# An attention and bilinear feed-forward kernel: the last matrix product by Strassen's scheme, every engine's instructions in a written order

## The chip, the cores and the metric

The kernel runs on one core of one Trainium2 chip. The metric is the device time of one execution in microseconds, lower being better. Five engines run side by side from queues of their own: TensorE (PE; its weight loads are shown apart as PEld), VectorE (DVE), ScalarE (ACT), GpSimd (POOL) and SyncE (SP, which here only issues the transfers). They meet through semaphores.

## The reference

For 8 batches of 8 heads, 576 positions, head size 64, a softmax over 32 memory slots turns keys and values into 32 memory rows per head. The queries attend to these 32 rows. The result is read as a 4608 x 512 matrix `x` and goes through a feed-forward layer without a nonlinearity other than a product.

```python
a = phi - np.max(phi, axis=2, keepdims=True)
a = np.exp(a)
a = a / (np.sum(a, axis=2, keepdims=True) + 1e-09)
k_m = np.einsum('bhsm,bhsd->bhmd', a, k)
v_m = np.einsum('bhsm,bhsd->bhmd', a, v)
...
attn = attn / (np.sum(attn, axis=-1, keepdims=True) + 1e-09)
return np.matmul(attn, v_m).astype(np.float32)
...
a = x @ w1
b = x @ w2
h = a * b @ w3
return (h @ w_out).astype(np.float32)
```

`d_ff` is 1024 and the output has 512 columns. The weights come as float64.

## The kernel before

Three things are folded. `w3 @ w_out` is one 1024 x 512 matrix, formed once at the start (`product`, in START). The values' memory rows are multiplied with `w1` and `w2` per batch (`memory_weights`, four steps M), so that the probabilities multiply the outcome directly. And each large product is taken in three passes on float32r numbers that are split in a high and a low half: high x high, high x low, low x high. A split (`split`, L110) is a copy that rounds, on ACT (L111), and a subtraction on DVE (L112).

After START, which brings in and converts the weights and does the attention of batch 0, the program runs over 8 batches. A batch has two stages:

- **A, 16 units** (`ab_unit`, L428). A unit makes 128 of the 1024 columns of `a` and of `b` for one half of the positions (288): 6 matmuls into PSUM bank `a`, 6 into `b` (L440). ACT copies `a` out (L449), DVE multiplies it with `b` into `gr` (L451), and `gr` is split into `gh` and `gl` (L454).
- **O, 16 parts** (`out_part`, L457). For each half of the positions and each 128 of the 512 output columns, 24 matmuls (8 slices of the 1024, three passes, L465) add up in one PSUM bank `o`. ACT copies it to `osb` (L470) and SP sends it off.

The attention of the next batch is spread among the units. Its steps are named in the tables FIRST (batch 0) and STEADY (the others): `top` (maximum of phi, L158), `exp` (L164), `norm`, `turn0` and `turn4` (transposes on PE, L180 and L184, copied out by ACT), `mem` (L194), `blocks` (L219, then four small DVE instructions), `sc` (scores, L234), `se`, `sn`, `pr` (softmax and split), `M` (L293 and a split). `C` converts one piece of the weights from float64 with two ACT and three DVE instructions (L372 to L377), `N` is an M of batch 0, `K` splits a piece of `w3 @ w_out`.

PE and SP follow the order in which the program is written, that is, these tables. The order on ACT and DVE is set by the compiler's scheduler, which moves instructions by its own estimate of when they become ready. POOL does nothing after the first microsecond. PSUM has eight banks: `a` and `b` twice each, `o` twice, and a pair `x` for the small work.

## Time and profile before

| | |
|---|---|
| median of 3 runs | 556.19 us (554.48 to 556.4) |
| profiled execution, first to last instruction | 554.0 us |
| PE busy | 538.2 us (97%), 4696 matmuls |
| DVE busy | 311.4 us (56%), 599 instructions |
| ACT busy | 253.7 us (46%), 522 instructions |
| POOL busy | 0.7 us, 6 instructions |
| mean granted TensorE clock | 0.997 |

The profiled execution's own time is known as its span alone. What lies around it is taken as the difference to the median, 2.2 us. In the trace the first A unit starts at 75.1 us, batch 0 ends at 142.7 us, and the batches after it take 59.6 us each. Busy times add up durations that overlap: a 288-column matmul is shown with 295 ns, but the next one starts 133 ns after it.

### The profile page before, as it was taken

How to read it: one execution, taken by the hardware profiler on the slowest of the kernel's cores; microseconds unless marked ns; L12 is line 12 of the kernel's file. 1: busy time of each engine (PE TensorE's matmuls, PEld its weight loads, DVE VectorE, ACT ScalarE, POOL GpSimd, SP SyncE). 2: the span in 40 equal slices, each digit the busy share in tenths (PEclk: the TensorE clock that was granted, in tenths of full speed). 3: DMA queues.
4: the chain of work that ended last, by engine and by line, in shares of the span. 5: the costliest groups of instructions: out<-in, count | busy, mean ns of one | idle time of the engine just before them, and what ended most of it. 6: DMA issues, size and time to landing. Idle time of an engine off the chain costs nothing.

```text
span 554.0 us, 11182 instructions
## 1 busy us (share of the span) xinstructions
PE 538.2 (97%) x4696; PEld 470.1 (85%) x4696; DVE 311.4 (56%) x599; ACT 253.7 (46%) x522; POOL 0.7 (0%) x6
## 2 busy tenths in 40 slices
PE   3999989999999999999999999999999999999997
PEld 1453458988999899989998899989998999899997
DVE  5887997637457624681558335762478155824500
ACT  5877784624544434452543444333544354424411
POOL 0000000000000000000000000000000000000000
PEclk9999999999999999999999999999999999999999
DMA  8999628008140511333043304050123200110011
GB/s 316 407 372 391 254 76 297 4 24 300 64 158 27 168 37 38 136 118 95 4 172 99 96 22 164 22 170 33 70 104 128 87 2 2 34 44 11 1 44 44
DMA packets 28819, 64.17 MB, mean 116 GB/s; under 512 B 2144, under 2 KB 10336, under 8 KB 28768
## 3 DMA queue, kind: packets, MB, share of 16 engines
q1 hardware_dynamic: 28768, 63.45, 32.7%
q8 instruction: 37, 0.61, 0.5%
q14 instruction: 14, 0.11, 0.1%
HBM read 54.00 MB, written 9.44 MB: 115 GB/s over the span
## 4 chain that ended last, share of the span: by engine, by line
PE 91%; DVE 4%; DMA 2%; ACT 1%; issue 1%; DVEq 0%; ACTq 0%
PE o L465 37%; PE a L440 18%; PE b L440 18%; PE x L194 3%; PE a L387 2%; PE b L387 2%; PE a L293 2%; PE x L293 2%; DMA raw<-in_w_out 1%; PE x L180 1%; PE b L293 1%; PE x L234 1%; DVE w L377 1%; DMA raw<-in_w3T 1%; DVE w L376 1%; PE o L387 1%
## 5 line engine op out<-in xcount | busy, mean ns | idle before, releaser
L465 PE MATMUL o<-gh,Wh 128*128 128x288 f32 x512 | 152.9, 299 | 0.0
L465 PE MATMUL o<-gl,Wh 128*128 128x288 f32 x512 | 151.1, 295 | 0.0
L465 PE MATMUL o<-gh,Wl 128*128 128x288 f32 x512 | 151.1, 295 | 0.0
L465 PEld LDWEIGHTS o<-gh,Wh 128*128 128x128 f32 x512 | 96.8, 189 | 11.9 <-issue 11.9
L451 DVE TENSOR_TENSOR gr<-b,a_sb 128x288 f32<-128x288 f32 x128 | 58.5, 457 | 84.2 <-PE b L440 80.9
L111 ACT CAST gh<-gr 128x288 fp32r<-128x288 f32 x128 | 55.4, 433 | 99.4 <-DVE gr L451 99.4
L465 PEld LDWEIGHTS o<-gl,Wh 128*128 128x128 f32 x512 | 96.3, 188 | 0.0
L465 PEld LDWEIGHTS o<-gh,Wl 128*128 128x128 f32 x512 | 96.2, 188 | 0.0
L112 DVE TENSOR_TENSOR gl<-gr,gh 128x288 fp32r<-128x288 f32 x128 | 58.5, 457 | 56.7 <-ACT gh L111 56.4
L440 PE MATMUL b<-ah,mh 128*128 128x288 f32 x256 | 75.6, 295 | 2.7 <-DVE Wl L112 2.7
L440 PE MATMUL a<-ah,mh 128*128 128x288 f32 x256 | 78.0, 305 | 0.0
L440 PE MATMUL a<-al,mh 128*128 128x288 f32 x256 | 75.9, 296 | 0.0
L440 PE MATMUL b<-al,mh 128*128 128x288 f32 x256 | 75.9, 296 | 0.0
L440 PE MATMUL b<-ah,ml 128*128 128x288 f32 x256 | 75.9, 296 | 0.0
L440 PE MATMUL a<-ah,ml 128*128 128x288 f32 x256 | 75.8, 296 | 0.0
L470 ACT COPY osb<-o 128x288 f32<-128x288 f32 x64 | 25.3, 395 | 82.8 <-PE o L465 71.5
L449 ACT COPY a_sb<-a 128x288 f32<-128x288 f32 x128 | 50.5, 394 | 8.0 <-PE a L440 7.4
L440 PEld LDWEIGHTS a<-ah,mh 128*128 128x128 f32 x256 | 48.4, 189 | 4.2 <-issue 2.0
L440 PEld LDWEIGHTS b<-ah,mh 128*128 128x128 f32 x256 | 48.4, 189 | 3.0 <-DVE Wl L112 3.0
L440 PEld LDWEIGHTS b<-ah,ml 128*128 128x128 f32 x256 | 48.5, 189 | 0.0
L440 PEld LDWEIGHTS a<-ah,ml 128*128 128x128 f32 x256 | 48.5, 189 | 0.0
L440 PEld LDWEIGHTS b<-al,mh 128*128 128x128 f32 x256 | 48.4, 189 | 0.0
(89 smaller groups left out, 649.1 us busy)
## 6 DMA issues: line engine op xcount, KB each, us to landing
kv<-in_kv SPq DMA_DIRECT2D x16, 1024.0 KB, 7.8
q<-in_qT SPq DMA_DIRECT2D x8, 1152.0 KB, 6.0
outT<-osb SPq DMA_DIRECT2D x64, 144.0 KB, 1.8
raw<-in_w3T SPq DMA_DIRECT2D x7, 1024.0 KB, 11.9
ph<-in_phiT SPq DMA_DIRECT2D x8, 576.0 KB, 4.0
raw<-in_w SPq DMA_DIRECT2D x4, 1024.0 KB, 17.2
raw<-in_w_out SPq DMA_DIRECT2D x3, 1024.0 KB, 10.5
kv<-in_w SPq DMA_DIRECT2D x3, 1024.0 KB, 14.5
```

The source lines that it names most:

```text
L111: nc.scalar.copy(out=hi, in_=src)
L112: nc.vector.tensor_tensor(out=lo, in0=src, in1=hi.bitcast(F32), op=ALU.subtract)
L180: nc.tensor.transpose(ps[:, c, t], v["ph"][:, t, at : at + P], ident)
L194: nc.tensor.matmul(ps[h * M : (h + 1) * M, t, : 2 * D], lhsT=v["a"][:, i, t, h * M : (h + 1) * M], rhs=kvt[i][:, (4 * t + h) * 2 * D : (4 ...
L234: nc.tensor.matmul(ps[t][g * M : (g + 1) * M], lhsT=km[b % 2][t * D : (t + 1) * D, g], rhs=v["q"][t * D : (t + 1) * D, g, n * HALF : (n + ...
L293: nc.tensor.matmul(ps[t][g * M : (g + 1) * M], lhsT=vm[b % 2][d, g], rhs=w12_sb[q][d, :, g], start=True, stop=True,)
L387: nc.tensor.matmul(pw[r][i], lhsT=x[:, i * P : (i + 1) * P], rhs=wos[k // half][:, k % half], start=k == 0, stop=k == NF - 1,)
L440: nc.tensor.matmul(p, lhsT=x[:, t, w, fc : fc + P], rhs=y[:, n, t * HALF : (t + 1) * HALF], start=i == 0, stop=i == len(todo) - 1,)
L449: nc.scalar.copy(out=a_sb, in_=ps[0])
L451: nc.vector.tensor_tensor(out=gr, in0=ps[1], in1=a_sb, op=ALU.mult)
L465: nc.tensor.matmul(v["p"], lhsT=x[f // half][:, f % half, oc], rhs=y, start=f == 0 and i == 0, stop=f == NF - 1 and i == 2)
L470: nc.scalar.copy(out=osb, in_=v["p"])
```

## The change

**The O stage** is done by Strassen's scheme in Winograd's form. The 576 x 1024 matrix G of one batch (`a` times `b`) is cut in four quarters (two halves of the positions, two halves of the 1024), `w3 @ w_out` in four as well, and seven products of quarters take the place of eight. A product is two units of 12 matmuls (`out_unit`), so the stage has 14 units instead of 16 parts. The sums of quarters of G (16 subtractions or additions of 128 x 288 a batch) are done by POOL (`ab_unit`, `sums`), those of the weights, once, by POOL and DVE in batch 0 (`weights_of_out`: K, T, V, D, E, F, G). Sums of products are formed partly in PSUM, by further matmuls on the same bank, partly by four ACT copies (`keep`) and four DVE additions (`result`) of 128 x 576 a batch, which feed four transfers of 288 KB instead of eight of 144 KB.

**The splits** no longer follow each A unit: `gr` goes whole into G, and the operand of each O unit is split when it is near (`high_part` on ACT, h; `low_part` on DVE, l), 14 splits of 128 x 576 a batch in place of 16 of 128 x 288, through four buffers for each half.

**PSUM** is now four pairs of banks: `ab` twice, `o` and `x`. An A unit takes one pair, which comes free when its product with `b` is done.

**The order** of ACT, DVE and POOL is written out too, after START. Each unit has a group: what its batch needs, from the tables, and one group of STREAM, the next batch's attention, if a running estimate of DVE's backlog allows (`ahead_slot`). Two of the four M now stand in the O stage of the batch before, two in the A stage of their own.

**Conversions** C are cut in three, so that the last four lie between the first A units.

```diff
-STEADY = """
-A top A exp A norm A A turn0 A A turn4 A A mem A A kv2 blocks A A A A A
...
+BATCH_A = "A | A | A | A | A M | A h0 | A | A l0 | A M | A h1 | A l1 | A | A h2 | A | A l2 | A h3"
...
+BATCH_O = """
+O h4 l3 | O p1 h5 l4 | O h6 l5 | O p4 h7 l6 | O h8 l7 | O C11 h9 l8 | O h10 l9 | O u2 h11 l10 | O h12 l11 | O h13 p5 l12 |
...
+STREAM = """
+top | exp | norm turn0 | turn4 | mem | blocks kv | sc0 | mx0 | sb0 ex0 | sc1 q | sm0 | mu0 mx1 | tr0 sb1 ex1 | ah0 |
...
+LIMIT = 2100
...
+    def pair_ab():
+        return ps_ab.tile([P, 2, 512], F32, name="ab")
+
+    def pair_o():
+        return ps_ox.tile([P, 2, 512], F32, name="o")
+
+    def pair_x():
+        return ps_ox.tile([P, 2, 512], F32, name="x")
...
+            both = (pair_o(), pair_x()) if r else (pair_ab(), pair_ab())
+            pw[r] = [x[:, i] for x in both for i in range(2)]
...
-    def keep(r, i):
-        if r == 1 and Wh[1] is None:
-            Wh[1], Wl[1] = w_half(1)
-        split(Wh[r][:, i], Wl[r][:, i], pw[r][i])
...
+        if step == "K":
+            nc.scalar.copy(out=c, in_=pw[0][i])
+        if step == "T":
+            nc.gpsimd.tensor_tensor(out=two, in0=two, in1=one, op=sub)
+            high(0, i, c)
+        if step == "V":
+            low(0, i, c, nc.gpsimd)
+        if step == "D":
...
+            high(1, i, pw[1][i])
+            nc.vector.tensor_tensor(out=two, in0=pw[1][i][:, OH:], in1=two, op=sub)
+        if step == "E":
+            low(1, i, pw[1][i], nc.vector)
+            nc.vector.tensor_tensor(out=t4[i], in0=pw[1][i][:, :OH], in1=two, op=sub)
+        if step == "F":
+            nc.gpsimd.tensor_tensor(out=one, in0=two, in1=one, op=sub)
+            high(3, i, t4[i], slice(0, OH))
+            high(2, i, c)
+        if step == "G":
+            low(3, i, t4[i], nc.gpsimd)
+            low(2, i, c, nc.gpsimd)
...
+    big = ctx.enter_context(tc.tile_pool(name="big", bufs=1, reuse_waits="tile"))
+    start(START[last:])
...
+        both = pair_ab()
...
         a_sb = big.tile([P, HALF], F32, name="a_sb", bufs=2)
-        nc.scalar.copy(out=a_sb, in_=ps[0])
-        gr = big.tile([P, HALF], F32, name="gr", bufs=2)
-        nc.vector.tensor_tensor(out=gr, in0=ps[1], in1=a_sb, op=ALU.mult)
-        gh = big.tile([P, HALF], F32R, name=f"gh{n}{f}")
-        gl = big.tile([P, HALF], F32R, name=f"gl{n}{f}")
-        split(gh, gl, gr)
-        g[n, f] = (gh, gl)
...
-            v["p"] = psum(ps_o, "o")[:, :HALF]
-        oc = slice(o * P, (o + 1) * P)
-        for f in range(part * NF // 2, (part + 1) * NF // 2):
-            gh, gl = g[n, f]
-            for i, (x, y) in enumerate(((Wh, gh), (Wl, gh), (Wh, gl))):
-                nc.tensor.matmul(
-                    v["p"], lhsT=x[f // half][:, f % half, oc], rhs=y, start=f == 0 and i == 0, stop=f == NF - 1 and i == 2
-                )
-        if part == 1:
-            osb = big.tile([P, HALF], F32, name="osb", bufs=3)
-            nc.scalar.copy(out=osb, in_=v["p"])
-            c = b * S + n * HALF
-            nc.sync.dma_start(out=outT[oc, c : c + HALF], in_=osb)
...
+        for k in range(half):
+            a, s3, s2, a12 = G[0, 0][:, k], G[1, 0][:, k], G[1, 1][:, k], G[0, 1][:, k]
+            if which == ("2a", "2b")[k // 2]:
+                gp(out=s2, in0=s2, in1=s3, op=ALU.subtract)
+            elif which == "1":
+                gp(out=a, in0=s2, in1=a, op=ALU.add)
+            elif which == "4":
+                gp(out=a12, in0=a12, in1=s2, op=ALU.subtract)
+
+    order = (1, 4, 2, 6, 5, 7, 3)
+    weights = {1: (0, 0), 5: (0, 1), 2: (1, 0), 3: (1, 1), 7: (2, 0), 6: (2, 1), 4: (3, 0)}
...
+    def high_part(m, G):
+        src = G[sources[order[m // 2]]][:, m % 2 * 2 : m % 2 * 2 + 2]
+        hi = big.tile([P, 2, HALF], F32R, name="sh", tag="sh", bufs=4)
+        nc.scalar.copy(out=hi, in_=src)
+        G["X", m] = [hi, None, src]
+
+    def low_part(m, G):
+        hi, _, src = G["X", m]
+        lo = G["X", m][1] = big.tile([P, 2, HALF], F32R, name="sl", tag="sl", bufs=4)
+        nc.vector.tensor_tensor(out=lo, in0=src, in1=hi.bitcast(F32), op=ALU.subtract)
+        done = {2: "2a", 3: "2b", 1: None, 5: "4"}.get(m)
+        if done:
+            sums(done, G)
+        if done == "2b":
+            sums("1", G)
...
+    def out_unit(b, m, G):
+
+        i, part = order[m // 2], m % 2
+        bank = "x" if i in (4, 5, 3) else "ab" if i == 2 else "o"
+        if part == 0 and i in (1, 4, 2, 5):
+            G[bank] = {"o": pair_o, "x": pair_x, "ab": pair_ab}[bank]()
+        ps = G[bank]
+        s, oc = weights[i]
+        hi, lo, _ = G["X", m]
+        for j in range(2):
+            jc = slice(oc * OH + j * P, oc * OH + (j + 1) * P)
+            for k in range(2):
+                for t, (x, y) in enumerate(((Wh, hi), (Wl, hi), (Wh, lo))):
+                    nc.tensor.matmul(
+                        ps[:, j, :HALF],
+                        lhsT=x[s][:, 2 * part + k, jc],
+                        rhs=y[:, k],
+                        start=i in (1, 4, 2, 5) and part == 0 and k == 0 and t == 0,
+                        stop=part == 1 and k == 1 and t == 2,
+                        skip_group_check=True,
+                    )
...
+    def keep(what, G):
+        c = G[what] = big.tile([P, 2, HALF], F32, name="c", tag="c", bufs=3)
+        nc.scalar.copy(out=c, in_=G["o" if what in ("p1", "u2") else "x"][:, :, :HALF])
+
+    def result(b, what, G):
+        bank, kept = {"C11": ("ab", "p1"), "C22": ("o", "p5"), "C21": ("o", "p4"), "C12": ("x", "u2")}[what]
+        c = G[kept]
+        nc.vector.tensor_tensor(out=c, in0=G[bank][:, :, :HALF], in1=c, op=ALU.add)
+        n, oh = int(what[1]) - 1, int(what[2]) - 1
+        at = b * S + n * HALF
+        dst = outT[oh * OH : (oh + 1) * OH, at : at + HALF].rearrange("(j p) s -> p j s", j=2)
+        nc.sync.dma_start(out=dst, in_=c)
...
+        for_b, group = ahead
+        if for_b > b + 2 or slot < ready_at or slot < first_slot:
+            return
...
+        cost = sum(columns(x) for x in group)
+        behind = size * for_b + spare - slot <= len(groups(STREAM)) - groups(STREAM).index(group)
+        if busy + cost > LIMIT and not behind:
+            return
+        bank = pair_x if in_a and b else pair_ab
+        busy = max(0, busy - sum(TENSOR.get(x, 0) for x in group)) + cost
...
+            for at, group in enumerate(todo_a + todo_o):
...
+                    elif what == "M":
+                        m_steps[b].pop(0)(pair_o)
...
+                if not in_a and b + 1 < B and m_steps.get(b + 1) and (b + 1, "blocks") in emitted:
+                    left = len(m_steps[b + 1]) - 2
+                    if left and (n_o >= 14 - 3 * left or busy + columns("M") < LIMIT):
+                        m_steps[b + 1].pop(0)(pair_ab)
+                        busy = max(0, busy - TENSOR["M"]) + columns("M")
+                        new = True
+                if group[0] != "O" or n_o != 5 or not new:
+                    ahead_slot(b, in_a)
...
+    ordered = {mybir.EngineType.Activation, mybir.EngineType.DVE, mybir.EngineType.Pool}
+    with tc.manual_schedule(engines=ordered):
+        batches()
```

Three places of the order. The first is PE in an O stage, at the second group of M steps. `x`, `a`, `b`, `o` and `ab` are PSUM banks; `w_1`, `w_2` the slices of the feed-forward weights. Before:

```order
L465 MATMUL o<-gh_2277,Wl_86 128x288
L465 MATMUL o<-gl_2278,Wh_85 128x288
L293 MATMUL x<-w_1_82,vm_80 32x512 x8
L293 MATMUL a<-w_2_83,vm_80 32x512
L293 MATMUL b<-w_2_83,vm_80 32x512
```

Now, in an O stage, at its second M:

```order
L567 MATMUL o<-sh,Wl_83 128x288
L567 MATMUL o<-sl,Wh_82 128x288
L316 MATMUL ab<-w_1_79,vm_76 32x512 x8
L567 MATMUL x<-sh,Wh_750 128x288
L567 MATMUL x<-sh,Wl_753 128x288
```

Before, three M follow each other (the rest of them stands behind the rows shown); now each M stands alone between two units of large matmuls. The scores, which were one run with an M, are in two runs. In all there are 44 places with small matmuls between the large ones before, 65 now, and 3072 large matmuls before, 2880 now.

The second is ACT around the exponential of phi (`ph<-ph,mx`), for one of the middle batches. Before, in the O stage, three output copies and five A units ahead of the transposes that need it:

```order
L470 COPY osb<-o 128x288 x2
L164 ACTIVATE ph,sm<-ph,mx 128x576 x2
L470 COPY osb<-o 128x288 x3
L449 COPY a_sb<-a 128x288
L111 CAST gh_3669<-gr 128x288
L449 COPY a_sb<-a 128x288
L111 CAST gh_3693<-gr 128x288
```

Now, in the A stage, and the copy behind the transposes is L192:

```order
L122 CAST mh_3578<-o 128x1024
L513 COPY a_sb<-ab 128x288
L541 CAST sh<-g_3395 128x576
L513 COPY a_sb<-ab 128x288
L175 ACTIVATE ph,sm<-ph,mx 128x576 x2
L513 COPY a_sb<-ab 128x288
L192 COPY a<-x 128x1024
L513 COPY a_sb<-ab 128x288
L541 CAST sh<-g_3398 128x576
```

The exponential moved to one A unit ahead of the transposes: between it and the transposes' copy stands one `a_sb`. On DVE its maximum stands directly behind the product of the tenth unit, on PE the transposes behind the twelfth.

The third is DVE at the end of START and the first A units. `al` is the low half of the probabilities, `ml` that of M, `Wl` that of `w3 @ w_out`. Before:

```order
L112 TENSOR_TENSOR Wl_475<-a,Wh_474 128x512
L112 TENSOR_TENSOR Wl_475<-o,Wh_474 128x512 x2
L112 TENSOR_TENSOR al<-at,ah 128x576
L372 TENSOR_SCALAR al<-q 128x1024
L377 ISA w_2_83<-w_2_83,ua 128x2048
L112 TENSOR_TENSOR Wl_475<-b,Wh_474 128x512
L112 TENSOR_TENSOR ml_488<-x,mh_487 128x1024
L451 TENSOR_TENSOR gr<-b,a_sb 128x288
L377 ISA w_3_84<-w_3_84,al 128x2048
```

Now:

```order
L279 TENSOR_TENSOR s_sb<-s_sb,ss_436 128x576
L292 TENSOR_TENSOR al<-at,ah 128x576
L285 STREAM_TRANSPOSE at<-s_sb 128x576
L292 TENSOR_TENSOR al<-at,ah 128x576
L123 TENSOR_TENSOR ml_479<-ab,mh_478 128x1024
L515 TENSOR_TENSOR g_487<-ab,a_sb 128x288
L390 TENSOR_SCALAR um<-kv_365 128x1024
L515 TENSOR_TENSOR g_487<-ab,a_sb 128x288
L399 TENSOR_SCALAR w_2_80<-w_2_80 128x1024
L400 ISA w_2_80<-w_2_80,um 128x2048
```

The splits of the second half of `w3 @ w_out` no longer stand ahead of the first product; the last four conversions (`um`) now stand behind it.

More of the change, by code (lines that the diff above doesn't have):

```diff
@@ L285, in memory_weights, with step @@
         ms = ready["M", b] = []
-        def step(q, banks):
-            one = None if banks else psum_pair()
-            ps = banks() if banks else [one[:, t] for t in range(NT)]
+        def step(q, bank):
+            ps = bank()
             for g in range(NG):
@@ L393, in product @@
             )
[L395 to L412 removed]
+    OH = DO // 2
@@ L413, in memory_attention__then__bilinear_ffn_kernel, with start @@
+    steps = {0: attention(0)}
+    m_steps = {0: memory_weights(0)}
+    todo = iter(range(len(tasks)))
+    now = []
+    def start(todo_list):
+        for what in todo_list:
             if what == "C":
-                next_tile()
+                for _ in convert(next(todo)):
+                    pass
             elif what[0] == "W":
```

290 lines of the change are left out of this document (179 added, 111 removed).

## The prediction

> **What bounds the kernel now.** First the busy times, the first part of the page:
>
> ```profile
> PE 538.2 (97%) x4696; PEld 470.1 (85%) x4696; DVE 311.4 (56%) x599; ACT 253.7 (46%) x522; POOL 0.7 (0%) x6
> ```
>
> PE is busy throughout, but its matmuls overlap in this count, so I go to the busy times by stage: the first A stage, then three whole batches (columns: length, then busy time and instructions of PE, PEld, DVE, ACT, POOL, then the granted clock).
>
> ```profile
> 80.50:108.60 28.10, 28.09 (x216) 25.76 (x217) 20.93 (x40) 16.40 (x37) 0.00 (x0) 0.94 0.43 148
> ...
> 202.60:262.30 59.70, 59.70 (x574) 55.67 (x573) 32.23 (x66) 25.06 (x59) 0.00 (x0) 1.00 0.28 91
> 262.30:321.90 59.60, 59.60 (x573) 55.58 (x572) 32.30 (x66) 25.13 (x59) 0.00 (x0) 1.00 0.27 90
> ```
>
> A batch lasts 59.6 us and PE never rests in it, while DVE and ACT work 32.3 and 25.1 us. So PE's instructions set the time, and the chain of waits (start, length, what) tells their price:
>
> ```profile
> 96.97 1.02 PE x L293 x16
> 97.99 0.99 PE a L440 x6
> 98.98 0.80 PE b L440 x6
> ...
> 171.31 1.59 PE o L465 x12
> ...
> 174.88 9.71 PE o L465 x72
> ...
> 184.60 1.02 PE x L293 x16
> ...
> 187.33 14.52 PE o L465 x108
> ...
> 525.39 25.47 PE o L465 x192
> ```
>
> The last row is an O stage with nothing in between: 192 matmuls at 25.47 / 192 = 0.1327 us, or 1.59 for a unit of 12. Of the 59.6 us, 384 x 0.1327 = 50.9 are large matmuls and 8.7 small ones.
>
> **The matmuls removed.** Seven products for eight: 24 fewer of 192 a batch, 192 in all, 192 x 0.1327 = **-25.5 us**. The built order has 2880 large matmuls for 3072, so that the change does not do what it says is no rival. Each keeps its weight load, so its price stays.
>
> **The small work in more places.** A lone M costs 1.02 us and the matmuls behind it 0.99 in place of 0.80: 1.21 us. Three in a row take 187.33 - 184.60 = 2.73 us, and the 108 matmuls behind them 14.52 for 14.33: 2.92 us. So an M is worth (2.92 - 1.21) / 2 = 0.855 us, and each entry into small work another 0.36. The run of two scores and an M takes 174.88 - 172.90 = 1.98 us, and the 72 matmuls behind it 0.16 more than 9.55: 2.14 in all, which leaves 0.46 for one score step. The order has 65 such entries for 44: 21 x 0.36 = **+7.6 us**. Below it could be nothing, were the entries hidden by waits; above, the rows give no more.
>
> **The end of START.** PE's instructions in order of time at the second A unit, and the chain there:
>
> ```profile
> 80.51 0.40 PE L440 MATMUL b<-ah,mh 128*128 128x288 f32 x1 [2.73 <-DVE Wl L112]
> ```
> ```profile
> 80.51 1.06 PE b L440 x6
> 81.56 1.38 PE a L440 x6
> 82.94 1.44 PE b L440 x6
> 84.38 1.28 PE x L293 x16
> ```
>
> PE waits 2.73 us for a bank that holds `w3 @ w_out` until the split on DVE, and then its matmuls take almost twice as long for a while (clock 0.94 in the stage): 0.26 + 0.58 + 0.64 + 0.26 = 1.75 more. With the pairs `o` and `x` holding that product until later, both go: **-4.5 us**. The start of the first unit, 75.1 us, is set by PE's own row of products and stays.
>
> By the Trainium skill (TensorE: Matmul & The Clock Gate, Part 1) the clock halves after an idle window of about 3.4 us and needs as long to return. The trace agrees in kind: 2.73 us sufficed here.
>
> In its place the second unit takes the pair of the second M of START, which DVE frees. Instructions of ACT and DVE in order of time, the first from behind the lone M above:
>
> ```profile
> 98.10 1.01 ACT L111 CAST mh<-x 128x1024 fp32r<-128x1024 f32 x1
> ```
> ```profile
> 80.37 1.21 DVE L112 TENSOR_TENSOR ml<-x,mh 128x1024 fp32r<-128x1024 f32 x1
> 81.51 0.45 DVE L451 TENSOR_TENSOR gr<-b,a_sb 128x288 f32<-128x288 f32 x1
> ```
>
> From M's start: the copy after 1.13, the subtraction after 2.15, done 1.14 later, 3.3 us. PE then has M and one unit behind it, 1.0 + 1.6 = 2.6. **+0.7 us.**
>
> **Batch 0.** These groups by line carry the rest:
>
> ```profile
> L451 DVE TENSOR_TENSOR gr<-b,a_sb 128x288 f32<-128x288 f32 x128 | 58.5, 457 | 84.2 <-PE b L440 80.9 <-ACT gh L111 1.9 <-PE x L184 0.9
> L449 ACT COPY a_sb<-a 128x288 f32<-128x288 f32 x128 | 50.5, 394 | 8.0 <-PE a L440 7.4
> L112 DVE TENSOR_TENSOR al<-at,ah 128x576 fp32r<-128x576 f32 x16 | 11.5, 755 | 0.6
> L111 ACT CAST ah<-at 128x576 fp32r<-128x576 f32 x16 | 10.7, 675 | 22.3 <-DVE at L269 22.3
> L373 ACT ACTIVATE w<-kv 128x1024 f32<-128x1024 f32 x3 | 3.5, 1157 | 0.2 <-DMA kv<-in_w 0.2
> L374 ACT ACTIVATE ua<-kv 128x1024 uint16<-128x1024 uint32 x2 | 2.8, 1392 | 0.0
> L112 DVE TENSOR_TENSOR Wl<-a,Wh 128x512 fp32r<-128x512 f32 x3 | 2.1, 686 | 1.4 <-ACT Wh L111 1.4
> L111 ACT CAST Wh<-a 128x512 fp32r<-128x512 f32 x3 | 1.8, 585 | 1.0 <-PE a L387 0.9
> L112 DVE TENSOR_TENSOR gl<-gr,gh 128x288 fp32r<-128x288 f32 x128 | 58.5, 457 | 56.7 <-ACT gh L111 56.4
> L111 ACT CAST gh<-gr 128x288 fp32r<-128x288 f32 x128 | 55.4, 433 | 99.4 <-DVE gr L451 99.4
> masks.py:199 POOL TENSOR_SCALAR_AFFINE_SELECT ident<-ident 128x128 f32<-128x128 f32 x1 | 0.3, 292 | 0.1
> masks.py:197 POOL MEMSET ident<- 128x128 f32 x1 | 0.2, 204 | 0.3 <-POOLq L536 0.3
> L536 POOL MEMSET const-uint8-127<- 128x1 uint8 x1 | 0.1, 102 | 0.0
> ```
>
> In the first ten A units ACT has ten copies (3.9), four conversions (4 x 2.55 = 10.2), four weight copies T (2.3) and two M (2.0): 18.5 us, PE 10 x 1.59 + 2 x 1.21 = 18.3. ACT has nothing to spare, and each T waits in ACT's queue for a subtraction on POOL, with the next unit's `a_sb` behind it, and behind that the pair of banks. POOL has no such row. From 102 ns for one element to 204 and 292 for 128, it does one element in 0.8 to 1.5 ns; 288 elements cost 0.33 us at the least and, with two inputs at the slower rate, 0.96 at most. I take 0.65, from between. Four waits of that: **+2.6 us** (0, if POOL is always ahead, to 5).
>
> In the last six units DVE has six products (2.7), one M (1.2), the weights' D and E (eight of 256 columns, estimated at 0.45 from the 288-column row, and four of 512: 6.3), three l (2.3) and the next maximum (1.35): 13.9 us, less 0.09 for each of 22 instructions that overlap (457 ns long, 0.37 apart): 11.9. PE has 6 x 1.59 and the first O unit, 11.1, and then stands at `turn0`, which needs the exponentials, 1.6 us behind the maximum: 13.5 - 11.1, and one h ahead of them on ACT, **+3.0 us** (1 to 5, and 1.75 more if the clock falls).
>
> **The other batches.** DVE loses 16 x 0.457 (gl) and gains 14 x 0.755 (l) and 4 x 0.755 (results): 38.6 us a batch. ACT loses 16 x 0.433 (gh) and 8 x 0.40 (osb), gains 18 x 0.675: 27.1. Neither bounds 57 us; what counts is one wait after another in the written order. The rows for the exponential:
>
> ```profile
> 313.35 1.35 DVE L158 TENSOR_REDUCE mx<-ph 128x2 f32<-128x1152 f32 x1 [3.71 <-DMA ph<-in_phiT]
> ```
> ```profile
> 314.79 0.78 ACT L164 ACTIVATE ph<-ph,mx 128x576 f32<-128x576 f32 x1 [2.74 <-DVE mx L158]
> ...
> 316.23 0.19 ACT L164 ACTIVATION_READ_ACCUMULATOR ph<-ph,mx 128x1 f32 x1
> ```
>
> I count from the end of the ninth A unit, where an M starts. Its subtraction ends at 3.3, the tenth product lets the maximum start at 3.7, the exponentials start 1.44 later and last 1.63: 6.8. PE has M and three units, 1.21 + 4.77 = 6.0, and stands 0.8 us at `turn0`. In the O stage the second M needs the pair of the first (3.3 after its start), and PE has M, scores and a unit to do: 0.855 + 0.46 + 0.36 + 1.59 = 3.27; with a semaphore's delay, 0.2. Together 1.0 us in each of batches 1 to 6: **+6.0 us** (0 to 18). Batch 7 prepares nothing. The eight copies and results of a batch have two or three O units' time (3.2 us and more) before PE needs their bank or their split; without that cover they would cost up to 0.755 each.
>
> **The end.** The chain and the transfers' rows:
>
> ```profile
> 550.93 0.40 ACT osb L470
> ```
> ```profile
> outT<-osb SPq DMA_DIRECT2D x64, 144.0 KB, 1.8
> ```
>
> A 576-column addition for this copy is 0.36 longer, and twice the bytes take up to 1.8 longer; I take 0.5. **+0.9 us.** SP's other transfers keep their distance: phi is fetched five groups ahead.
>
> **Sum:** 554.0 - 25.5 + 7.6 - 4.5 + 0.7 + 2.6 + 3.0 + 6.0 + 0.9 = 544.8 us of span. The median is 2.2 above the span shown, which I keep: **547.0 us**, 1.7% faster.
>
> **Rivals.** *The new waits are hidden:* PE's list alone, 544.8 - 2.6 - 3.0 - 6.0 = 533.2, **535.4 us**. For it speaks that DVE and ACT have 19 and 30 us to spare in each batch; against it, that the waits follow from single chains, not from load.
>
> *The waits are twice as long* (11.6 more): 558.6, **no measurable change**. For it: an order fixed by hand passes each delay on to all that is queued behind it.
>
> *POOL holds up DVE.* In each O stage ten POOL instructions run beside the splits l4 to l8, which read two operands from SBUF. If each of the five waits out one POOL instruction, 5 x 0.65 = 3.3 us come on this path: PE reaches the ninth unit seven units and four small steps after the first, 11.1 + 3.7 = 14.8. DVE by then has the first M (done at 3.3), a second (1.2), four transposes of scores (4 x 0.46, by the 288-column row), nine instructions of 576 columns (6.8): 9.8, less 15 x 0.09 of overlap, so 11.8; waiting for the second M's copy and the second scores costs it some 1.8, which leaves 1.2. The rest, 2.1, comes in each of 7 batches, and in batch 0 four conversions hold two such instructions each, 5.2: 547.0 + 14.7 + 5.2 = **566.9 us**, slower. From 0.47 us a wait on (8 and 7 x 5 of them, less 7 x 1.2, make 12) it passes 559. Nothing in this trace shows POOL and DVE together, as POOL is idle. The Trainium skill (SBUF — State Buffer, Who interferes with whom) states just this: an instruction of DVE with two SBUF inputs and one of GpSimd that reads SBUF shut each other out for their whole length. No row here can test it; it gives the rival its chance.
>
> **How the numbers follow.** This kernel's three runs lie within 0.35%, so I call 0.5% no change: 553.4 to 559.0. Forecast (540 to 553.4) 0.48; hidden waits (under 540) 0.28; doubled waits (553.4 to 559) 0.13; POOL and other losses (above 559) 0.11. So faster 0.76, same 0.13, slower 0.11. The range 535 to 561 leaves out some 0.07 below and 0.10 above.
>
> **What would show it.** Right: a batch of 57.5 us plus about 1, with idle PE before `turn0` released by ACT's exponential; small work in 65 places at the old prices; no 2.73 us wait at the second A unit; idle PE in batch 0 of 5 to 8 us. POOL's instructions near 0.65 us, and DVE's l as long as 0.755 us: much longer ones speak for the third rival. Wrong: batches of 57.5 us without idle PE (first rival), or DVE as the releaser of most of PE's O units.

## The result, and the profile after

The changed kernel takes **569.49 us** (569.38 to 570.24) against 556.08 us for the kernel before in the same comparison: a ratio of 1.0255, 95% interval 1.0234 to 1.0276. It is slower by 2.5%, where 547.0 us, 1.6% faster, was forecast. Three of the runs below had one execution that took far longer than its others (1795.53, 710.0 and 857.05 us); their times are given without it.

The page of the profiled execution (span 567.7 us), busy time of each engine:

```profile
PE 532.0 (94%) x4504; PEld 448.6 (79%) x4504; DVE 365.9 (64%) x598; ACT 276.5 (49%) x465; POOL 141.2 (25%) x154
PEclk9999998979999999999999999999999999999999
```

The matmuls are gone as foreseen: 192 fewer, and PE is busy 6.2 us less. But its share fell from 97% to 94%, and the granted clock has two dips in batch 0 (the 8 and the 7; a third, at the start of batch 1, lies across two slices and does not show). Busy times by stage, before (START, batches 0 and 1, then batch 6 and the last one; columns as in the prediction, and behind the clock the share and the GB/s of the transfers):

```profile
0.00:75.10 75.10, 65.23 (x283) 28.34 (x283) 59.96 (x91) 55.47 (x62) 0.70 (x6) 1.00 0.86 322
75.10:142.70 67.60, 64.86 (x618) 58.24 (x611) 44.58 (x82) 32.15 (x66) 0.00 (x0) 0.97 0.45 153
142.70:202.60 59.90, 59.88 (x573) 55.62 (x572) 32.37 (x69) 26.93 (x64) 0.00 (x0) 1.00 0.27 90
...
441.10:500.00 58.90, 58.90 (x568) 54.88 (x567) 30.63 (x63) 23.32 (x54) 0.00 (x0) 1.00 0.06 22
500.00:554.00 54.00, 50.85 (x385) 50.61 (x383) 14.67 (x32) 15.40 (x41) 0.00 (x0) 1.00 0.08 26
```

and after (START, batches 0, 1 and 2, and the last one):

```profile
0.00:74.90 74.90, 64.81 (x284) 28.32 (x285) 54.21 (x82) 48.69 (x55) 1.43 (x7) 1.00 0.86 325
74.90:154.00 79.10, 63.76 (x548) 54.98 (x547) 56.50 (x85) 43.52 (x74) 37.36 (x35) 0.94 0.36 121
154.00:216.50 62.50, 60.27 (x548) 54.28 (x549) 38.28 (x68) 27.35 (x50) 14.40 (x16) 0.97 0.25 83
216.50:275.60 59.10, 58.53 (x549) 52.57 (x548) 37.87 (x66) 27.35 (x50) 14.41 (x16) 1.00 0.27 91
...
512.10:567.70 55.60, 50.49 (x393) 48.05 (x391) 27.46 (x41) 20.19 (x37) 16.00 (x16) 0.98 0.09 30
```

Nearly the whole loss is in two places: batch 0 is 11.5 us longer than before and batch 1 is 2.6 us longer. Batches 2 to 5 gain only 0.5 us each, batch 6 is 0.2 us longer than before (59.1 us), and the last one 1.6. By my terms batch 0 should have lasted 64.2 us (67.6 - 3.2 for 24 matmuls + 0.4 for one more entry - 4.5 + 0.7 + 2.6 + 3.0, less 2.4 for two M that now stand in the last batch), batch 1 58.8, a later one 58.5 (59.6 - 3.2 + 1.1 + 1.0), the last one 54.8 with those two M. So of the 22.9 us of span by which I was too low, 14.9 are lost in batch 0, 3.7 in batch 1, 3.7 in the five after it (1.3 of them in batch 6, which was shorter than the others before) and 0.8 in the last; START is 0.2 us shorter.

PE's instructions in order of time, with the longest stand of the A stage, that before `turn0`, and the first two of batch 1 (a stand is idle time of PE, in brackets with its releaser):

```profile
89.33 0.40 PE L505 MATMUL ab<-ah,mh 128*128 128x288 f32 x1 [3.40 <-DVE g L515]
...
119.22 0.47 PE L191 MATMUL ab<-ident,ph 128*128 128x128 f32 x1 [4.92 <-ACT ph L175]
...
153.28 0.40 PE L505 MATMUL ab<-ah,mh 128*128 128x288 f32 x1 [2.25 <-ACT ah L288]
154.07 0.40 PE L505 MATMUL ab<-al,mh 128*128 128x288 f32 x1 [0.40 <-DVE al L292]
```

The first comes from the A stage. ACT's queue there:

```profile
82.76 1.40 ACT L393 ACTIVATE ua<-kv 128x1024 uint16<-128x1024 uint32 x1
87.86 0.62 ACT L425 CAST Wh<-raw 128x512 fp32r<-128x512 f32 x1 [3.70 <-POOL raw L437]
88.39 0.39 ACT L513 COPY a_sb<-ab 128x288 f32<-128x288 f32 x1
```

and POOL's in the same time:

```profile
82.49 1.23 POOL L520 TENSOR_TENSOR g<-g,g 128x288 f32<-128x288 f32 x1 [42.29 <-DVE g L515]
83.68 1.74 POOL L428 TENSOR_TENSOR Wl<-raw,Wh 128x512 fp32r<-128x512 f32 x1
85.38 1.77 POOL L520 TENSOR_TENSOR g<-g,g 128x288 f32<-128x288 f32 x1
87.11 0.72 POOL L437 TENSOR_TENSOR raw<-raw 128x256 f32<-128x256 f32 x1
88.56 1.29 POOL L428 TENSOR_TENSOR Wl<-raw,Wh 128x512 fp32r<-128x512 f32 x1 [0.73 <-ACT Wh L425]
89.80 1.24 POOL L437 TENSOR_TENSOR raw<-raw 128x256 f32<-128x256 f32 x1
94.66 0.81 POOL L520 TENSOR_TENSOR g<-g,g 128x288 f32<-128x288 f32 x1 [3.62 <-DVE g L515]
```

The copy Wh (step T) waits 3.70 us for POOL's subtraction L437, which itself takes 0.72 us. What it waits out are the three instructions ahead of it in POOL's written order, a sum of G, a split V and another sum. The first of these could not start before DVE's product g of the unit just finished. Behind Wh in ACT's queue stands `a_sb`, which the bank of PE's next unit needs. So a wait travels from DVE over POOL and ACT to PE.

The stand of 4.92 us is `turn0`. The end of batch 1's attention is late too: `ah` for PE's first A unit of batch 1 is what ends the stand of 2.25 us. After the first two of these stands and after the last the clock is half for a while, for 10.2 us in batch 0 and 3.4 in batch 1. PE is busy for 8.1 and 3.4 us of that time; if that work takes twice as long as at full clock, it costs 4.1 and 1.7 us (an estimate).

### The profile page after: what moved, and what is told of

It reads as the page before. It is cut to its first block, busy times and chain, and to the rows that moved or that the text cites. A ratio compares the mean times of both kernels' runs of the same rounds, so it can differ in the third digit from the quotient of the medians.

```text
span 567.7 us, 10851 instructions
## 1 busy us (share of the span) xinstructions
PE 532.0 (94%) x4504; PEld 448.6 (79%) x4504; DVE 365.9 (64%) x598; ACT 276.5 (49%) x465; POOL 141.2 (25%) x154
## 4 chain that ended last, share of the span: by engine, by line
PE 78%; DVE 9%; ACT 7%; DMA 2%; POOL 1%; issue 1%; DVEq 0%; ACTq 0%
PE ab L505 29%; PE x L567 13%; PE o L567 11%; PE ab L567 4%; PE ab L411 4%; PE ab L316 4%; DVE ml L123 3%; ACT mh L122 3%; PE o L316 3%; PE o L411 3%; PE x L411 2%; PE x L205 2%; DVE mx L169 2%; ACT ph L175 2%; DMA raw<-in_w_out 1%
## 5 line engine op out<-in xcount | busy, mean ns | idle before, releaser
L505 PE MATMUL ab<-ah,mh 128*128 128x288 f32 x512 | 155.9, 305 | 8.4 <-DVE g L515 5.5
L505 PE MATMUL ab<-al,mh 128*128 128x288 f32 x512 | 152.7, 298 | 2.0 <-DVE al L292 2.0
L505 PE MATMUL ab<-ah,ml 128*128 128x288 f32 x512 | 151.6, 296 | 0.0
L515 DVE TENSOR_TENSOR g<-ab,a_sb 128x288 f32<-128x288 f32 x128 | 58.2, 455 | 112.0 <-ACT a_sb L513 112.0
L505 PEld LDWEIGHTS ab<-ah,mh 128*128 128x128 f32 x512 | 96.8, 189 | 26.2 <-DVE g L515 19.8
L547 DVE TENSOR_TENSOR sl<-g,sh 128x576 fp32r<-128x576 f32 x112 | 93.0, 842 | 16.2 <-ACT sh L541 16.1
L505 PEld LDWEIGHTS ab<-al,mh 128*128 128x128 f32 x512 | 96.9, 189 | 3.7 <-DVE al L292 3.7
L505 PEld LDWEIGHTS ab<-ah,ml 128*128 128x128 f32 x512 | 97.2, 190 | 0.0
L541 ACT CAST sh<-g 128x576 fp32r<-128x576 f32 x112 | 74.9, 675 | 33.8 <-PE x L567 11.9
L567 PE MATMUL o<-sh,Wh 128*128 128x288 f32 x192 | 58.4, 304 | 0.0
```

The costliest lines, as they stand in the source:

```text
L505: nc.tensor.matmul(both[:, w, :HALF], lhsT=x[:, t, w, fc : fc + P], rhs=y[:, n, t * HALF : (t + 1) * HALF], start=i == 0, stop=i == len(to ...
L515: nc.vector.tensor_tensor(out=G[n, f // half][:, k], in0=both[:, 1, :HALF], in1=a_sb, op=ALU.mult)
L541: nc.scalar.copy(out=hi, in_=src)
L547: nc.vector.tensor_tensor(out=lo, in0=src, in1=hi.bitcast(F32), op=ALU.subtract)
L567: nc.tensor.matmul(ps[:, j, :HALF], lhsT=x[s][:, 2 * part + k, jc], rhs=y[:, k], start=i in (1, 4, 2, 5) and part == 0 and k == 0 and t == ...
```

## The experiments

Two theories. **Chain:** PE waits in batch 0 for single chains of instructions that the written order makes long (POOL's subtraction in ACT's queue, the maximum and exponentials in front of `turn0`, the attention dealt out too late). **Load:** DVE and POOL shut each other out and have too much to do in batch 0, whatever the order. My third rival, POOL holding up DVE in every batch, is a form of the second.

### The subtractions of T in START

```diff
 if step == "K":
     nc.scalar.copy(out=c, in_=pw[0][i])
+    nc.gpsimd.tensor_tensor(out=two, in0=two, in1=one, op=sub)
 if step == "T":
-    nc.gpsimd.tensor_tensor(out=two, in0=two, in1=one, op=sub)
     high(0, i, c)
```

> The four subtractions of the weights' step T on POOL are issued in START, right behind the copies K, where POOL is idle; everything else as in the changed kernel (569.5 us). Chain theory: in batch 0 ACT stands 3.70, 0.97 and 2.12 us for these subtractions, with the next unit's copy a_sb behind it, and PE stands for that copy; without them the A stage of batch 0 is 4 to 6 us shorter and all behind it comes earlier: 564 us (563 to 566). Load theory (POOL and DVE shut each other out, so that the same number of instructions takes the same time wherever it stands): 568 us or more, the A stage at most 1.5 us shorter.

565.26 us (565.25 to 565.90), 4.2 us less than the changed kernel, ratio to the kernel before 1.0169 (1.0131 to 1.0208). This is within what chain expected, near the upper end of its times. The four instructions still exist; only their place in the queue is another.

### T and V in START

```diff
 if step == "K":
     nc.scalar.copy(out=c, in_=pw[0][i])
-if step == "T":
     nc.gpsimd.tensor_tensor(out=two, in0=two, in1=one, op=sub)
     high(0, i, c)
-if step == "V":
     low(0, i, c, nc.gpsimd)
```

(all of it now belongs to K, in START; the steps T and V do nothing in batch 0)

> The steps T and V as a whole (four subtractions and four splits on POOL, four copies on ACT) stand in START behind the copies K; PE's and DVE's orders stay as in the changed kernel (569.5 us). Chain theory: over the run with T's subtractions alone in START (565.6 us) POOL's queue in front of the A stage is free and DVE's conversions no longer stand beside POOL's splits (four of them took 0.4 to 0.9 us longer than the others): 563.5 us (562 to 565); the stand before turn0 stays, since mx stays where it is. Load theory, in which POOL's work costs the same in any place: 565 to 567 us, START ends later.

564.12 us (563.69 to 564.63), ratio 1.0153 (1.0134 to 1.0171). This is the time that chain expected. The step from the run before, 1.1 us, is not clear of noise, as the two ratios' intervals overlap. The stand before `turn0` stays, 4.84 us. START ends 1.3 us later, which the shorter A stage pays for.

### No sums of G on POOL

```diff
-            if f < half:
-                gp(out=low, in0=top, in1=low, op=ALU.subtract)
...
-        if done:
-            sums(done, G)
-        if done == "2b":
-            sums("1", G)
```

> The 16 subtractions and additions of combined products on POOL (four between the first A products, twelve in the O stage) are left out of every batch, so the products multiply uncombined terms. Exclusion theory (my third rival: each of POOL's instructions makes a split on DVE wait, and PE pays for it in every batch): the batches from the third on shorten by about 2 us each, 57 in place of 59.13 us, and the time is 553 us or less. Chain theory: the splits shorten (from 0.84 to 0.75 us in the mean) but PE does not wait for them: the later batches stay within 0.2 us of 59.13; batch 0 gains 1 to 4 us, as the subtractions stand in front of T in POOL's queue: 567 us (565 to 569).

The kernel leaves out all 16 sums of a batch. 566.78 us (565.80 to 567.23), ratio 1.0192 (1.0152 to 1.0233). The stages from the third batch on, and the splits:

```profile
214.12:273.26 59.14, 58.56 (x550) 52.61 (x549) 37.04 (x66) 27.37 (x50) 0.00 (x0) 1.00 0.26 91
...
L546 DVE TENSOR_TENSOR sl<-g,sh 128x576 fp32r<-128x576 f32 x112 | 83.7, 758 | 20.7 <-ACT sh L540 20.6
```

against this row of the changed kernel:

```profile
L547 DVE TENSOR_TENSOR sl<-g,sh 128x576 fp32r<-128x576 f32 x112 | 93.0, 842 | 16.2 <-ACT sh L541 16.1
```

This settles the third rival. POOL does hold up the splits, by 84 ns in the mean, but without POOL a later batch still lasts 59.14 us. DVE has the time to spare there. Most of the 2.7 us gained lies in batch 0 (76.7 us in place of 79.1).

### Batch 0 in the scheduler's order

```diff
+            if b == 1:
+                tc_order.enter_context(tc.manual_schedule(engines=ordered))
...
-    with tc.manual_schedule(engines=ordered):
+    with ExitStack() as tc_order:
         batches()
```

> In batch 0 alone ACT, DVE and POOL are ordered by the scheduler, as the kernel before has it throughout; from batch 1 on the written order stays. PE's and SP's orders do not change. If the written order is what passes POOL's delays on to the copies a_sb, batch 0 gains several of the 11.5 us by which it is longer than before: 563 us (559 to 566). If the work itself (POOL's and DVE's instructions shutting each other out) sets the end of batch 0, no more than 1.5 us: 568 to 571 us.

563.56 us (561.80 to 563.73), ratio 1.0125 (1.0084 to 1.0167). The same instructions in another order save 5.9 us, as chain has it. It is a mixed gain: the stand before `turn0` is gone, but in this order the second A unit stands 6.15 us for an M's split, and a later one 1.95 us for a product.

### Dealing from the tenth group

```diff
-    first_slot = 13
+    first_slot = 9
```

> The next batch's attention is dealt out from the 10th group of batch 0 on in place of the 14th; nothing else changes. Chain theory: the attention of batch 1 starts too late in batch 0, which costs PE 5.2 us before turn0, 2.3 + 0.4 us before the first and 1.6 us before the fifth A unit of batch 1, and the half clock behind each stand. With four groups' more time most of it goes: 561 us (558 to 565), batch 1 near 59.5 us in place of 62.5. Load theory (DVE has no room there: 7.7 of 8 us busy before turn0): the stand moves to another place of batch 0, 567 us or more; only the 4 us at the start of batch 1 could go.

569.50 us (569.12 to 569.83). Nothing follows for either theory: a second condition, the budget of columns (`LIMIT`), held every step where it was, and the built order did not change by one instruction. The run is a second measurement of the changed kernel.

### The maximum and the exponentials earlier in batch 0

```diff
-    first_slot = 13
+    first_slot = 10
...
+        first = for_b == 1 and ("top" in group or "exp" in group)
-        if busy + cost > LIMIT and not behind:
+        if not first and (slot < 13 or busy + cost > LIMIT and not behind):
```

with T and V in START and POOL's steps `low(2, i, c)` moved behind all of G.

> As with T and V in START, and the maximum mx and the exponentials for batch 1 are dealt out three or more groups of batch 0 earlier, with turn0 and all of PE's order where it was; POOL's splits of the third weight (not needed before the seventh O unit) stand behind those of the fourth. Chain theory: PE's 5.2 us before turn0, the half clock behind it, and the stands of 2.3, 0.4 and 1.6 us at the start of batch 1 (the same chain, late) go, up to 11 us, less what DVE's later D and E steps cost: 555 us (552 to 559), batch 1 near 59.5 us. Load theory (DVE was 7.7 of 8 us busy before turn0): the stand moves behind the next instruction of DVE, 560 us or more.

562.14 us (561.39 to 563.99), ratio 1.0122 (1.0095 to 1.0148): 2.0 us less than with T and V alone, where chain expected 9; load had said 560 us or more, so by its time alone this run speaks for load. Its trace does not: the stand before `turn0` is gone, and so are the clock's dips in the profiled execution (1.00 in batch 0). But the rest of the chain stayed: PE stands 2.75 us for `kvm`, and at the start of batch 1 the same 2.25, 0.40 and 1.57 us as before. That was my error: these are not an echo of `turn0`. Each step of the attention has a place of its own in the order, one a unit, and the last ones come late because the first places are late.

### The whole chain earlier

```diff
-    first_slot = 13
+    first_slot = 11
...
+        first = for_b == 1 and groups(STREAM).index(group) < 5
-        if busy + cost > LIMIT and not behind:
+        if not first and busy + cost > LIMIT and not behind:
```

(maximum and exponentials are no longer moved apart; PE's order changes: `turn0` two units earlier, `mem` and the scores three)

> T and V in START and POOL's splits in the order of need, as in the run that gave 562.1 us, and the first five groups of batch 1's attention are dealt out of batch 0 from its 12th group on whatever the columns' budget says, so that turn0 stands two units earlier in PE's order, mem and scores three. Late-chain theory (the stands of 2.25, 0.4 and 1.6 us at the start of batch 1 with the half clock behind them are the end of a chain that started too late): they go, 557 us (555 to 559), less only what mem waits for its keys. Load theory (DVE has as much as it can do from 75 to 150 us): the same time lost in other stands of batch 0, 561 us or more.

558.88 us (558.00 to 559.09), ratio 1.0051 (1.0034 to 1.0068). Late chain was right this time: the stands at the start of batch 1 are gone, and batch 1 takes the 59.14 us of a later batch. The chain of waits, its A stages of batches 1 and 2:

```profile
147.71 8.22 PE ab L504 x60
...
206.85 8.22 PE ab L504 x60
```

### Seven splits of batch 0 on POOL

```diff
+        engine = nc.gpsimd if b == 0 and m in (0, 1, 2, 10, 11, 12, 13) else nc.vector
-        nc.vector.tensor_tensor(out=lo, in0=src, in1=hi.bitcast(F32), op=ALU.subtract)
+        engine.tensor_tensor(out=lo, in0=src, in1=hi.bitcast(F32), op=ALU.subtract)
```

> As the run with the earlier dealing, and in batch 0 alone the splits l0 to l2 and l10 to l13 are made by POOL in place of DVE, 5.3 us less for DVE, about 7 x 1.4 us more for POOL. Load theory: batch 0 shortens by 3 to 5 us against the run with the earlier dealing. Late-chain theory: within 1 us of it, since DVE only passes on what it waits for. If POOL's splits shut DVE out for as long as they last, nothing is gained either.

559.99 us (559.18 to 560.52), ratio 1.0075 (1.0060 to 1.0090): 1.1 us slower than without. From 75 to 147.5 us DVE is busy 47.96 us in place of 55.43, and nothing is won. But the run does not test load cleanly, as PE now waits for one of the splits on POOL:

```profile
124.31 0.40 PE L567 MATMUL x<-sl,Wh 128*128 128x288 f32 x1 [3.42 <-POOL sl L547]
```

The run without conversions, further down, takes work off DVE without handing it to another engine.

### M two units earlier

```diff
-... A h0 | A | A l0 | A M | A h1 ...
+... A h0 | A M | A l0 | A | A h1 ...
```

> In batches 1 to 7 the second M of the A stage stands two units earlier, and the dealing of the next batch's steps moves one unit forward with it; batch 0 unchanged. If the stand of 0.5 us before turn0 in each later batch comes from M's split standing in front of the maximum on DVE, as the prediction's term has it, it goes: batches from the third on 58.6 us in place of 59.14, 566.5 us (565.5 to 567.5). If it comes from the maximum's place in the dealing itself, it stays: 569 to 570 us.

572.03 us (571.56 to 573.62), ratio 1.0300 (1.0276 to 1.0323). The stand before `turn0` stayed, and DVE's instructions in order of time show why:

```profile
290.74 1.23 DVE L123 TENSOR_TENSOR ml<-o,mh 128x1024 fp32r<-128x1024 f32 x1 [1.25 <-ACT mh L122]
...
293.44 0.46 DVE L515 TENSOR_TENSOR g<-ab,a_sb 128x288 f32<-128x288 f32 x1 [0.44 <-ACT a_sb L513]
293.81 1.34 DVE L169 TENSOR_REDUCE mx<-ph 128x2 f32<-128x1152 f32 x1
```

M's split is done 1.8 us before the maximum starts. The maximum waits in DVE's queue for the product g of its own unit, and from there `turn0` is only two units of PE away. In the changed kernel M's split did stand directly in front of this product, but it held it up by less than 0.1 us: the product's other operand, `a_sb`, was ready at 235.53 us, and the product started at 235.60.

A later batch lasts 59.62 us here (A starts at 216.15 and 275.77) in place of 59.14, as the dealing moved by one unit with M. That is a sum of four things, read from PE's starts. The way through `turn0` takes 0.25 us longer, with an `h` now ahead of the exponentials in ACT's queue. The second M's pair no longer makes PE wait, 0.22 less. A score step starts 0.35 later than a lone one does, right behind the small DVE instructions of `blocks`. And this score step no longer stands beside an M, which makes one more entry into small work: 0.12.

### An empty step between the exponentials and turn0

```diff
-top | exp | norm turn0 | turn4 | mem ...
+top | exp | gap | norm turn0 | turn4 | mem ...
```

> The changed kernel with one empty step between exp and turn0 in the list that is dealt out: turn0, turn4 and mem stand one unit later on PE, all other places on PE stay. Moving M two units earlier did not take the stand before turn0 away (0.23 and 0.43 us stayed), so it comes from the distance of two units (3.2 us) between the maximum's place and turn0's, against 1.27 + 1.63 us of maximum and exponentials and what DVE does before them. With three units it goes: 0.4 to 0.5 us in each of batches 1 to 6, in batch 0 the exponentials come one group earlier for another 0 to 2 us: 566.5 us (564.5 to 567.5). If the stand comes from ACT's queue, it only moves behind the next unit: 569 to 570 us.

561.25 us (559.43 to 561.86), ratio 1.0093 (1.0073 to 1.0114): 8.2 us for one empty word in a table, more than expected. The windows of batches 0, 1 and 2:

```profile
74.90:150.40 75.50, 63.34 (x556) 55.51 (x549) 57.47 (x85) 43.37 (x74) 37.91 (x35) 0.95 0.36 129
150.40:211.90 61.50, 59.79 (x547) 54.21 (x548) 38.11 (x67) 27.25 (x50) 14.37 (x16) 0.97 0.25 83
211.90:270.20 58.30, 58.16 (x549) 52.60 (x548) 37.90 (x66) 27.25 (x50) 14.36 (x16) 1.00 0.27 92
```

A later batch takes 58.30 us in place of 59.14, 0.84 less, and batch 0 takes 75.5 in place of 79.1, because the exponentials come one group earlier there. In the changed kernel's trace and this one's, 3.6 of the gain lies in batch 0, 1.0 in batch 1 and 0.84 in each of the five after it. So the distance on PE between a step and its consumer is the lever.

### Sums of the parts

Moving M earlier was joined to the first set of changes in one run, with the last result in two halves:

> All together: T and V in START, mx and exponentials of batch 0 earlier, POOL's splits in the order of need, M two units earlier, and the last result added and sent in two halves. If the parts add up: the time of the run with the first three, less 3 us for the six stands before turn0, less 0.5 to 1.2 us at the end: 551 us (548 to 555), below the kernel before. If they cover the same stands: within 1.5 us of the run with the first three.

566.28 us (564.22 to 568.23), ratio 1.0187 (1.0148 to 1.0225). It does not add up: a later batch lasts 59.62 us here too, as in the run with M alone, which is 2.9 us in six batches. The rest of the excess is not accounted for.

> T and V in START, POOL's splits in the order of need, the earlier dealing in batch 0, seven of its splits on POOL, the empty step before turn0 in the later batches and the last result in two halves. If what the parts save adds up: the time of the run with seven splits on POOL, less 2.5 us for the empty step, less 0.5 to 1.2 us at the end: about 552 us (549 to 556). Otherwise within 1.5 us of that run.

554.29 us (553.57 to 557.01), ratio 0.9980 (0.9967 to 0.9993), near the forecast of the sum, though the seven splits on POOL cost in it: PE stands 3.41 us for one of them. The next two runs leave these splits on DVE and put the empty step into every batch:

```diff
-    first_slot = 13
+    first_slot = 10
-top | exp | norm turn0 | ...
+top | exp | gap | norm turn0 | ...
+        first = for_b == 1 and groups(STREAM).index(group) < 6
...
+        cuts = [slice(0, 1), slice(1, 2)] if b == B - 1 and what == "C12" else [slice(0, 2)]
```

With T and V in START:

> T and V in START, POOL's splits in the order of need, batch 1's attention dealt out of batch 0 from its 11th group on, the empty step between exp and turn0 in every batch, the last result in two halves; all splits l on DVE. If the parts add up: 558.9 us of the run with the earlier dealing, less 5.0 for the empty step in six later batches (0.84 each, measured), less 1.2 at the end, less 2 to 3 for the stand of 1.96 us before turn0 in batch 0 and its half clock: 550 us (548.5 to 552). If in batch 0 DVE's load sets the pace, the last part comes to nothing: 552.7 us (551.5 to 554).

**552.48 us** (552.40 to 553.75), ratio 0.9947 (0.9933 to 0.9961): 0.5% faster than the kernel before, 3.0% below the changed one. It came out at the upper of the two values: the last 2 to 3 us expected in batch 0 did not come. I had put that value down to load; the run without conversions, below, speaks against it.

With only T's subtractions in START:

> As the first of these three, but only the four subtractions T of POOL stand in START; T's copies on ACT and V's splits on POOL stay in the A stage of batch 0. START then ends 1.3 us earlier (73.7 us in place of 75.0 in the kernel with T and V there); if POOL's splits V beside the conversions cost the A stage less than that, this is the faster of the two by up to 1 us; in the kernels with the old dealing it was the slower one by 1.5 us (565.6 against 564.1), and if that holds here too, it is 1 to 2 us slower.

553.53 us (551.26 to 554.97), ratio 0.9958 (0.9943 to 0.9973). Not told apart from the other. The windows of the profiled execution, which was its fastest (551.26 us; START, batches 0, 1, 2, and the last):

```profile
0.00:74.90 74.90, 65.21 (x284) 28.32 (x284) 54.90 (x82) 48.77 (x54) 4.02 (x10) 1.00 0.87 325
74.90:145.20 70.30, 59.96 (x557) 52.65 (x550) 57.66 (x84) 43.48 (x74) 35.21 (x32) 1.00 0.38 130
145.20:203.50 58.30, 58.16 (x550) 52.60 (x549) 38.44 (x68) 27.28 (x50) 14.38 (x16) 1.00 0.29 96
203.50:261.80 58.30, 58.16 (x550) 52.60 (x549) 37.91 (x66) 27.28 (x50) 14.38 (x16) 1.00 0.27 92
495.00:549.50 54.50, 50.45 (x393) 48.00 (x391) 27.51 (x42) 20.21 (x37) 16.00 (x16) 0.99 0.09 30
```

Batch 0 is down from 79.1 to 70.3 us at full clock. Is the rest load?

### Without DVE's part of the conversions

```diff
+        if i < FIRST_LATE:
             nc.vector.tensor_scalar(out=y, in0=y, scalar1=3, scalar2=None, op0=ALU.logical_shift_left)
             nc.vector.tensor_tensor(out=y, in0=y, in1=u, op=ALU.add)
```

(the same for the instruction that takes the sign)

> The same kernel, with DVE's three instructions of each of the four conversions in batch 0 left out (twelve instructions, some 11 us of DVE), so half of the weights of M is wrong; ACT's instructions of the conversions and all transfers stay. Load theory (what is left of batch 0's excess over a later batch comes from DVE's conversions standing between the products g and the splits): batch 0 shortens by 6 us or more. Chain theory (PE waits for single chains M, exponential, split, whatever DVE has to do beside): 2 us or less.

550.76 us (two runs, 550.59 and 550.92), ratio 0.9912 (0.9892 to 0.9931): 1.7 us for 11 us of DVE, which is what chain expected (2 us or less, load 6 or more). So load is not most of what is left. In this run too PE stands before `turn0` (1.63 us, for g) and before an M of the O stage (2.38 us, for the split of the M before it), as in the run with only T's subtractions in START (1.63 and 2.39 us). What the remaining chains of batch 0 would give was not tried.

## Why the prediction was wrong

**What held.** The matmuls: 192 fewer, and a unit of 12 still costs 1.59 us. The end of START: the old stand of 2.73 us is gone, the second A unit waits for M's pair as I counted (0.64 us). The later batches' waits: 0.84 before `turn0` where I had 0.8, and about 0.24 at the second M's pair where I had 0.2. The path to the first of these held step by step: M's split done 3.4 us after M's start (3.3 forecast), the maximum started at 3.7, the exponentials 1.4 later. That M's split was needed for it did not: with the split out of the way the stand stayed, as two units between the maximum and `turn0` are too few in any case. An entry into small work held near its 0.36: a lone M still takes 1.22 us in all and a lone score step 0.85, where my prices give 1.21 and 0.82. The third rival's mechanism is real, but its place was not: POOL and DVE hold each other up, and no later batch is longer for it. That its 566.9 us came near 569.5 is luck, as other things added up to it.

**What failed, in order of size.** The steps that failed are the waits of batch 0, at `turn0` and at the T steps: both terms were far too small, and the first chain was not followed into batch 1.

*Batch 0, "then stands at `turn0`, ... +3.0 us".* I counted DVE's work against PE's and took the difference. Measured: 4.92 + 0.28 us of stand, and half clock for 6.83 us behind it, which I had named beside the sum but not put in. For what comes after, the sum has nothing. I looked at the table up to `turn0` and did not follow the same chain on to `ah` and `al`, which batch 1's first and fifth unit wait for (2.25, 0.40 and 1.57 us, with half clock between). All steps for batch 1 are dealt one a unit from the 14th group on, so the last of them fall into batch 1 itself; the order showed that, and I did not read it to the end. The whole chain two to three units earlier, with POOL's splits in the order of need, gave 5.2 us more than T and V in START alone (564.1 to 558.9).

*Batch 0, "Four waits of that: +2.6 us".* I let each T wait for one subtraction of 0.65 us. It waits for everything ahead in POOL's queue: 3.70, 0.97 and 2.12 us, 6.8 in all. The bound "0 to 5" was too low. T and V in START took back 5.4 us of the whole.

*POOL's price.* 0.65 us was taken for 288 columns; undisturbed they take 0.79 to 0.81, and beside DVE up to 1.77. The upper bound, 0.96, held for POOL alone only.

*An M with a score step behind it.* A later batch's list: 59.14 us, less 47.8 for 360 matmuls, less 0.84, 0.24 and 0.20 of stands, is 10.1 for the small work where my prices give 9.8. The rest lies in one place: M and the score step behind it take 1.95 us in all, not 0.36 + 0.855 + 0.46 = 1.68. Why, no run shows. The 0.20 is a short stand at the fifth unit which I had not foreseen.

*The end, "+0.9 us".* From PE's last matmul to the end it takes 5.1 us (562.6 to 567.7) where it took 3.1 (550.9 to 554.0): 2.0. I charged 0.5 of up to 1.8 us for the larger transfer, and the upper bound was right. In two halves it is 4.0 us (545.5 to 549.5).

The rival "the waits are twice as long" (558.6) was the nearest in kind, and even it had too little: batches 0 and 1 alone were 18.6 us over the forecast. My range ended at 561 because each wait had been bounded by itself, none by the queue it stood in.

## What to carry to other kernels

When an order is written by hand on all engines, count a wait as all that stands ahead of its releaser in that engine's queue, not as the releaser's own duration, and follow a late chain to its last consumer, across the border of the loop. Between a step and its consumer on the busiest engine leave as many units of that engine's work as the chain is long: here one more unit, an empty word in a table, was worth 8.2 us, while taking 11 us of work off DVE gave 1.7. Work that is ready early (T, V) belongs where its engine is idle.

## What the runs showed of the hardware

POOL and DVE shut each other out, by kind of instruction. In the changed kernel's batch 0 a POOL subtraction of 256, 288 and 512 columns took from 0.72, 0.79 and 1.26 us up (from 0.74 and 1.29 us, an estimate: 2.15 ns a column and 0.19 us beside), and up to 1.70, 1.77 and 1.79 us beside certain instructions of DVE. DVE's and POOL's instructions there:

```profile
80.82 1.22 DVE L400 CUSTOM_DVE_ANT_0 w<-w,um 128x2048 uint16<-128x2048 uint16 x1 [0.22 <-ACT um L393]
...
82.97 0.44 DVE L515 TENSOR_TENSOR g<-ab,a_sb 128x288 f32<-128x288 f32 x1
...
84.40 2.10 DVE L400 CUSTOM_DVE_ANT_0 w<-w,ua 128x2048 uint16<-128x2048 uint16 x1
...
115.16 0.91 DVE L547 TENSOR_TENSOR sl<-g,sh 128x576 fp32r<-128x576 f32 x1
115.99 1.34 DVE L169 TENSOR_REDUCE mx<-ph 128x2 f32<-128x1152 f32 x1
117.25 0.44 DVE L515 TENSOR_TENSOR g<-ab,a_sb 128x288 f32<-128x288 f32 x1
117.62 2.09 DVE L547 TENSOR_TENSOR sl<-g,sh 128x576 fp32r<-128x576 f32 x2
```

The addition L400 (two operands from SBUF) took 1.22 us before POOL's first instruction and 2.10 beside it, the splits 0.91 and 1.05 where they take 0.75. The product g, one operand of which is in PSUM, kept its 0.44 to 0.46 us, and the maximum, with one operand, its 1.34 (1.35 before), though POOL was busy all through. One operand is not enough in each case: the shift L399 took 0.69 us before POOL began (at 79.91) and 0.93 beside it (at 83.33). The Trainium skill (SBUF — State Buffer, Who interferes with whom) states this rule: a DVE instruction with two inputs from SBUF contends with a GpSimd instruction that reads SBUF, one with at most one such input does not, outside the 2-port modes that `tensor_scalar`, the kind of L399, can enter. These figures agree with it.

What lowers the clock can be read from the traces. In the changed kernel half clock begins at 90.52, 117.83 and 155.37 us and lasts 3.41, 6.83 and 3.41 us. The starts lie 27.31 and 37.54 us apart, 8 and 11 times 3.413. So in this trace the clock is set once in each stretch of 3.41 us, wherever the stands lie. The stretches ahead of the first and the third start, each with the one behind it:

```profile
87.11:90.52 3.41, 1.20 (x9) 1.20 (x10) 1.71 (x3) 2.24 (x4) 2.68 (x4) 1.00 0.00 0
90.52:93.93 3.41, 2.99 (x22) 0.98 (x20) 2.01 (x3) 2.43 (x4) 0.52 (x1) 0.50 0.00 0
...
151.96:155.37 3.41, 1.69 (x10) 1.48 (x11) 2.52 (x5) 1.25 (x2) 0.00 (x0) 1.00 0.45 157
155.37:158.78 3.41, 3.41 (x17) 3.41 (x16) 1.12 (x2) 0.40 (x1) 0.00 (x0) 0.50 0.00 0
```

PE was busy for 0.35 and 0.50 of the stretches ahead. With the grid laid through fifteen of the traces, 33 stretches at full clock had PE busy for less than 0.48 of their length, and all were followed by half clock. Of those above 0.505 none was, and the six between went either way. So PE need not rest for a whole stretch: half of one is enough, and what counts is how the stands fall on the grid, not the length of the last one. In the run with the maximum and exponentials earlier in batch 0, PE had the same stands of 2.25 and 0.40 us, and the clock stayed full:

```profile
75.00:142.00 67.00, 58.32 (x540) 49.68 (x540) 51.39 (x76) 40.38 (x68) 28.77 (x28) 1.00 0.39 136
142.00:205.00 63.00, 58.21 (x543) 51.78 (x542) 39.84 (x69) 27.39 (x50) 14.41 (x16) 1.00 0.25 86
```

There the stands fell across two stretches, in which PE was busy 1.80 and 2.39 of 3.41 us. That they did is luck, and the clock differs from one execution to the next: the four of that kernel had mean clocks from 1.000 to 0.994 and took from 561.39 to 563.99 us. One stretch at half clock costs up to 1.7 us, half its length (an estimate), so a difference of 1 or 2 us between two kernels here can be one such stretch.
